# Two more pairs of down tiles as 2x2 block products in seven, on the first side of a fused attention and GLU block

## The chip, the cores and the metric

The kernel runs on one core of a Trainium2 chip. The metric is the device time of one execution in microseconds (us), as a median over several runs. One execution was also recorded by the hardware profiler; its rows give every instruction's start and duration. Engines are named as in the profile: PE multiplies matrices (PEld loads its stationary operand), DVE and POOL do elementwise work, ACT does elementwise work with a scale or function and most copies out of PSUM, SP issues DMA transfers. Each engine takes its instructions strictly in the order in which they were written.

## The reference

x is 2048 tokens of 512 numbers, all in float32. What is computed, with `ln` a layer norm without weights:

```python
sa, ca, ga, sb, cb, gb = (silu(c) @ w_mod) in six rows of 512
h = ln(x) * (1 + ca) + sa
x = x + ga * linear_attention(h, wqkv, wo)        # 32 heads of 16, phi(t) = elu(t) + 1 + 1e-6
h = ln(x) * (1 + cb) + sb
x = x + gb * (((h @ w_gate) * (h @ w_up)) @ w_down)   # 512 -> 1376 -> 512
```

## The kernel before

**Products in three passes.** The matrix products run on a shortened float32 type. So an operand X is split into a high part (ACT rounds it) and a low part (DVE or POOL subtracts the high part from X), and a product is three matmuls: high by high, high by low, low by high. Each split is thus one ACT instruction and one subtraction.

**Two sides.** The tokens are four chunks of 512 (j = 0 to 3 are four tiles of 128 tokens in a chunk). The GLU part works on two chunks at a time: the first side is chunks 0 and 1, the second side chunks 2 and 3. The hidden dimension of 1376 is cut into eleven f tiles (ten of 128, the last of 96). A **stage** here is one call of `block` (L1050 on), for one side and one f tile: the gate and up products of two chunks are seen as a 2x2 block product and done in seven products instead of eight (Winograd's form). The seven are called a11, s1, s2, a12, s3, a22, s4 in the code's order, each of 6 matmuls of 128x512 (L1057). They run in four PSUM banks a to d that all stages use in turn. On the way ACT copies b out of a, c out of b, then u2 (from b), g (from a) and u3 (from c); DVE adds c22 = d + u3 (L1113) before s4 may accumulate into d, and c12 = d + u2 (L1122) behind s4, then multiplies gate by up (L1083, twice). So the next stage's s1, which overwrites d, waits for L1122, and its a22, which accumulates into c, waits for the copy u3 (L1063).

The first side's stages 0 to 10 take the f tiles 2, 3, 4, 5, 6, 7, 8, 9, 0, 1, 10 in this order (`groups_of`, `order`). They begin at 206 us of the span; the second side follows at 373 us.

**The down product, two ways.** Where a group of f tiles is not *paired*, each h is split (L206, L207), and `down` (L1137) multiplies it for one or two f tiles at a time: 24 matmuls of 128x512 in each stage of the following group (L1146 to L1148), into four banks of the pool `ps_acc`, from which DVE adds into x (L1153, 128x512). Where two f tiles are *paired*, two chunks by two f tiles are again a 2x2 block product in seven (`Pair` from L1165, `pair_steps`). Its left operands are a11, a21 (first f tile), a12, a22 (second) and four sums s1 to s4 of them (L1182), split in L1168 and L1172; its right operands are the two rows of w_down and four sums of them, made on POOL (L1207) from rows that DVE has scaled by gb (L1280), and split in L1217 (ACT) and L1218 (DVE on the first side). A pair's seven steps are done for j = 0, 1 and again for j = 2, 3, 84 matmuls of 128x256 in all (L1226). A step b starts from a copy of step a's bank that ACT makes (`seed`, L1063 acc<-acc), and after most steps DVE adds a 128x256 result into x (L1253). Before the change, only tiles 0 and 1 are paired on the first side, and all full tiles on the second.

**Order.** There is no scheduler: every engine runs in the order of the code. `at` names points between the seven products of a stage ("s1" is behind s1, "pe" and "mid" lie around a22, "s4" is behind s4), and lists of jobs are run at each: the loading, summing and splitting of the next f tile's gate and up weights (`right_load`; `right_sums`, L1002 on POOL; `right_split`, L1013 and L1016 on ACT and L1020 on POOL), the down work, `trickle` (preparation of the second side's operands: sums L953 on DVE, splits L206 and L207), and the table `early`, which holds the end of the attention part: `y_a`/`y_b` (output projection of token tiles 12 to 15, L871 and L881), `turned` (L846, L850, L854) and the layer norm of chunks 2 and 3 (`ln2_x` L277, `ln2_turn` transposes L284 into a `ps_acc` bank, `ln2_f` L925 on ACT, which empties that bank).

`ps_acc` has four banks; `y_a`, `turned`, `ln2_turn`, `down` and the pair steps all take from it. A new use takes the bank that was given free the longest ago in the code's order, and waits for its last reader.

Of the kernel before, what the change touches and what calls it, by code (L numbers as in the profile page):

```python
# [22 lines left out]
def tile_adaln_block(  # L23
# [50 lines left out]
    def B(tag, shape=(P, D), dt=F32):  # L74

        return T(tiles, tag, shape, dt)

    def acc_bank():
        return T(ps_acc, "acc")
# [155 lines left out]
    def cut(pair, a, b):  # L235
        return pair[0][:, a:b], pair[1][:, a:b]
# [605 lines left out]
    def turn_a(i, of=bank):  # L842
        tps[i] = of()
        phi = phq.pop(i)
        for k in range(KD):
            nc.tensor.transpose(tps[i][:, k * P:(k + 1) * P], phi[:, k * P:(k + 1) * P], ident)  # L846

    def turn_h(i):
        pqs[i] = (B("xh", dt=F32R), B("xl", dt=F32R))
        nc.scalar.activation(pqs[i][0], tps[i], AF.Copy)  # L850

    def turn_l(i):
        h, l = pqs[i]
        nc.vector.tensor_tensor(l, tps.pop(i), f32(h), op=ALU.subtract)  # L854
# [8 lines left out]
    def y_a(i):  # L863
        pq = pqs.pop(i)
        fresh = i not in seeded
        if fresh:
            yps[i] = acc_bank()
        for k in range(KD):
            (ah, al), (bh, bl) = cut(pq, k * P, (k + 1) * P), wp[k]
            for n, (x, y) in enumerate(((ah, bh), (ah, bl), (al, bh))):  # L870
                nc.tensor.matmul(yps[i], x, y, start=fresh and k + n == 0,  # L871
                                 stop=k == KD - 1 and n == 2, skip_group_check=True)

    def y_b(i):
        ch, j = divmod(i, NJ)
        ps = yps.pop(i)
        if i in seeded:
            nc.scalar.activation(xts[ch][j], ps, AF.Copy)
            norm2[ch].stats(j, of=ps)
        else:  # L880
            nc.vector.tensor_tensor(xts[ch][j], xts[ch][j], ps, op=ALU.add)  # L881
            norm2[ch].stats(j)
# [36 lines left out]
    def ln2_turn(ch, *ks, of=bank):  # L919
        norm2[ch].transpose(*ks, of=of)  # L920

    def ln2_f(ch, *ks):
        for k in ks:
            f = B("f")
            nc.scalar.activation(f, norm2[ch].ps[k], AF.Identity, scale=cb[:, k:k + 1], bias=sb[:, k:k + 1])  # L925
            norm2[ch].ps[k] = None
            if ch < 2:
                plain[ch, k] = f
            else:
                nc.sync.dma_start(kept[ch, k], f)  # L930
# [457 lines left out]
    def turned(i):  # L1388
        turn_a(i, of=acc_bank)
        turn_h(i)  # L1390
        turn_l(i)

    def ln2_x(ch, *js):
        norm2[ch].xhat(*js)

    def ln2_r(ch, a=0, b=NJ):
        norm2[ch].rstd_of(a, b, True)

    def ln2_m(ch, a=0, b=NJ):
# [12 lines left out]
        (1, "pe"): [lambda: y_a(14), lambda: y_b(14)],  # L1412
        (1, "mid"): [lambda: ln2_turn(2, 0, 1, of=acc_bank)],
        (1, "s4"): [lambda: ln2_f(2, 0, 1)],
        (2, "s1"): [lambda: turned(15), lambda: ln2_turn(2, 2, 3, of=acc_bank)],
        (2, "s2"): [lambda: ln2_f(2, 2, 3)],
        (2, "pe"): [lambda: y_a(15), lambda: y_b(15), lambda: ln2_r(3)],
        (3, "s2"): [lambda: ln2_x(3, 0)],
        (3, "s3"): [lambda: ln2_x(3, 1)],
        (3, "mid"): [lambda: ln2_x(3, 2)],  # L1420
        (3, "s4"): [lambda: ln2_x(3, 3)],
        (4, "s1"): [lambda: ln2_turn(3, 0, 1, of=acc_bank)],
        (4, "s2"): [lambda: ln2_f(3, 0, 1)],
        (5, "s1"): [lambda: ln2_turn(3, 2, 3, of=acc_bank)],
        (5, "s2"): [lambda: ln2_f(3, 2, 3)],
    }
# [4 lines left out]
    groups = groups_of[1]  # L1431
    tail = groups[-1][-1]
    POINTS = ("s1", "s1", "a12", "a12", "pe", "pe", "s4")
    paired = {(0, g) for g in [4]} | {(1, g) for g in range(len(groups))}
    pair_of = {(s, f): (s, g) for s, g in paired for f in groups_of[s][g][:2]}
    same = {(1, 0): (0, 4)}
    points = POINTS
# [3 lines left out]
    for n, (s, g, f) in enumerate(order):  # L1441
        groups = groups_of[s]
# [72 lines left out]
        if was and was[:2] in paired and was[2] == groups_of[was[0]][was[1]][1]:  # L1515
            of, p = was[0], pairs[was[:2]]
# [87 lines left out]
```

## Time and profile before

| | |
|---|---|
| runs: median (lowest to highest) | 553.79 us (553.67 to 554.7) |
| span of the profiled execution, first to last instruction | 552.4 us |
| median of the runs less that span | 1.4 us |
| PE busy | 545.8 us, 99% |
| DVE, ACT, POOL busy | 432.2, 299.5, 176.8 us |
| stage 1 (second tile of the first group) | 221.5 to 235.1 us |
| stage 4 and stage 5 | 269.1 to 285.0, 285.0 to 300.8 us |
| stage 6 and stage 7 | 300.8 to 315.8, 315.8 to 330.8 us |
| stages 9 and 10 (end of the one pair before, and what follows it) | 345.7 to 373.1 us |

Times in the profile are microseconds from the first instruction. In a row of the timeline stand the start, the duration (of all instructions that it merges, with their count behind the x), engine, line, what is written and read, the size, and in brackets the idle time of the engine just before with what ended it. PE instructions overlap in the records (a 128x512 matmul lasts 390 ns, but the next starts after some 227 ns), so what a matmul costs is read from starts.

### The profile page before, as it was taken

The page shows a single profiled execution, that of the slowest core. Times are in us where ns is not written, and L with a number is a line of the kernel's source. Part 1 is how long each engine was busy: PE and PEld are TensorE (multiplying, and loading weights), DVE is VectorE, ACT ScalarE, POOL GpSimd, SP SyncE. Part 2 cuts the span into 40 slices and gives each one's busy share as a digit, 9 for nine tenths or more (in the row PEclk, how much of TensorE's full clock was granted, in tenths as well). Part 3 has the DMA queues.
Part 4 walks back from the last instruction along what each step waited for, and adds up shares of the span by engine and source line. Part 5 has one row for each costly group of instructions (what it writes and reads, how often), then busy time and mean ns, then how long its engine had stood idle before and what let it go on. Part 6 is the DMA issues. An engine that isn't in the chain of part 4 may idle for free. (4 is left out here: it accounts for less than half of the span.)

```text
span 552.4 us, 8146 instructions
## 1 busy us (share of the span) xinstructions
PE 545.8 (99%) x2775; PEld 460.1 (83%) x2775; DVE 432.2 (78%) x794; ACT 299.5 (54%) x535; POOL 176.8 (32%) x180
## 2 busy tenths in 40 slices
PE   8999999999999999999999999999999999999997
PEld 6888888888888888888888888878888888888886
DVE  6878779978998998865655767797577877879696
ACT  4876857456467876654545355463243534453540
POOL 2000000003527646353556644540002524242400
PEclk9999999999999999999999999999999999999999
DMA  8910224203230045195888634289786534342004
GB/s 256 373 57 1 76 77 152 77 0 77 78 115 2 0 154 189 39 316 180 285 286 274 222 123 163 87 312 391 231 259 218 173 131 138 129 146 86 1 0 153
DMA packets 58512, 83.24 MB, mean 151 GB/s; under 512 B 6564, under 2 KB 23720, under 8 KB 58472
## 3 DMA queue, kind: packets, MB, share of 16 engines
q1 hardware_dynamic: 56544, 81.16, 44.1%
q10 hardware_dynamic: 1928, 1.58, 0.9%
q8 instruction: 22, 0.36, 0.3%
q14 instruction: 18, 0.15, 0.1%
HBM read 53.02 MB, written 29.69 MB: 150 GB/s over the span
## 5 line engine op out<-in xcount | busy, mean ns | idle before, releaser
L1057 PE MATMUL bank<-h,w 128*128 128x512 f32 (+1 forms) x924 | 221.6, 391 | 0.2 <-POOL w L1020 0.2
L1057 PEld LDWEIGHTS bank<-h,w 128*128 128x128 f32 (+1 forms) x924 | 168.2, 186 | 36.2 <-POOL w L1020 0.6
L1063 ACT ACTIVATE bank<-bank 128x512 f32<-128x512 f32 (+2 forms) x46 | 26.2, 571 | 122.7 <-PE bank L1057 122.5
L1253 DVE TENSOR_TENSOR x<-acc,x 128x256 f32<-128x256 f32 x132 | 48.0, 414 | 13.7 <-PE acc L1226 13.1
L1226 PE MATMUL acc<-w,kh 128*128 128x256 f32 x308 | 57.1, 282 | 0.0
L1226 PEld LDWEIGHTS acc<-w,kh 128*128 128x128 f32 x308 | 50.6, 190 | 3.7
L1020 POOL TENSOR_TENSOR w<-raw,w 128x256 fp32r<-128x256 f32 (+3 forms) x22 | 24.7, 1121 | 73.7 <-ACT w L1013 64.1
L219 PE MATMUL bank<-w,h 128*128 128x512 f32 x112 | 44.1, 394 | 0.0
L221 PE MATMUL bank<-w,h 128*128 128x512 f32 x112 | 43.7, 390 | 0.0
L220 PE MATMUL bank<-w,h 128*128 128x512 f32 x112 | 43.6, 390 | 0.0
L1226 PE MATMUL acc<-w,kl 128*128 128x256 f32 x154 | 43.5, 283 | 0.0
L871 PE MATMUL acc<-w,xh 128*128 128x512 f32 x128 | 40.7, 399 | 0.0
L712 POOL TENSOR_TENSOR f<-h,zb 128x512 f32<-128x512 f32 x12 | 17.5, 1468 | 62.9 <-ACT zb L692 48.9
L262 POOL TENSOR_TENSOR rstd<-ve,half 128x4 f32<-128x4 f32 (+3 forms) x12 | 11.2, 935 | 81.4 <-DVE ve L259 68.0
L1083 DVE TENSOR_TENSOR phi<-bank,g 128x512 f32<-128x512 f32 (+1 forms) x22 | 15.1, 687 | 25.2 <-PE bank L1057 25.2
L1063 ACT ACTIVATE u<-bank 128x512 f32<-128x512 f32 (+1 forms) x44 | 26.1, 594 | 15.4 <-PE bank L1057 15.2
L1113 DVE TENSOR_TENSOR g<-bank,u 128x512 f32<-128x512 f32 (+1 forms) x22 | 15.2, 689 | 21.2 <-ACT u L1063 19.9
L1020 POOL TENSOR_TENSOR w<-t,w 128x512 fp32r<-128x512 f32 (+1 forms) x22 | 29.6, 1346 | 0.0
L1146 PE MATMUL acc<-w,kh 128*128 128x512 f32 (+1 forms) x76 | 29.6, 390 | 0.0
L1147 PE MATMUL acc<-w,kh 128*128 128x512 f32 (+1 forms) x76 | 29.6, 390 | 0.0
L1148 PE MATMUL acc<-w,kl 128*128 128x512 f32 (+1 forms) x76 | 29.6, 389 | 0.0
L277 ACT ACTIVATE n<-x,nmr,rstd 128x512 f32<-128x512 f32 x31 | 23.6, 808 | 10.9 <-DVE nmr L267 10.7
(204 smaller groups left out, 1187.0 us busy)
## 6 DMA issues: line engine op xcount, KB each, us to landing
right<-w SPq DMA_DIRECT2D x56, 256.0 KB, 3.7
w<-right SPq DMA_DIRECT2D x56, 256.0 KB, 4.3
x<-in_A_x_dram SPq DMA_DIRECT2D x22, 256.0 KB, 5.2
raw<-in_w_mod_dram SPq DMA_DIRECT2D x22, 256.0 KB, 3.7
raw<-in_B_w_down_dram SPq DMA_DIRECT2D x18, 256.0 KB, 3.0
side_s<-h SPq DMA_DIRECT2D x16, 256.0 KB, 2.6
h<-side_s SPq DMA_DIRECT2D x16, 256.0 KB, 5.3
raw<-in_A_wqkv_dram SPq DMA_DIRECT2D x12, 256.0 KB, 6.2
```

What stands on the lines that cost most here:

```text
L219: nc.tensor.matmul(ps, ah, bh, start=begin and i == 0, stop=False)
L220: nc.tensor.matmul(ps, ah, bl, start=False, stop=False)
L221: nc.tensor.matmul(ps, al, bh, start=False, stop=end and i == n - 1)
L871: nc.tensor.matmul(yps[i], x, y, start=fresh and k + n == 0, stop=k == KD - 1 and n == 2, skip_group_check=True)
L1020: sub = lambda out, x, y: (on or nc.gpsimd).tensor_tensor(out, x, f32(y), op=ALU.subtract)
L1057: mm = lambda x, y, **kw: nc.tensor.matmul(ps, x[:, k], y, skip_group_check=True, **kw)
L1063: nc.scalar.activation(out, x, AF.Copy)
L1146: nc.tensor.matmul(dn[j], hh[:n, a:b], dh[:n], start=i == 0, stop=False)
L1147: nc.tensor.matmul(dn[j], hh[:n, a:b], dl[:n], start=False, stop=False)
L1148: nc.tensor.matmul(dn[j], hl[:n, a:b], dh[:n], start=False, stop=i == n_of - 1)
L1226: mm = lambda x, y, **kw: nc.tensor.matmul(ps, x[:, a:b], y, skip_group_check=True, **kw)
L1253: nc.vector.tensor_tensor(xt[:, halves[at]], banks[b][m], xt[:, halves[at]], op=ALU.add)
```

## The change

The set `paired` gains the groups 0 and 2 of the first side, f tiles 2, 3 and 6, 7. Their down products go from `down` to `Pair`. In `early`, `y_a(15)` moves from "pe" of stage 2 to "s3", the two sets of transposes of chunk 2 behind it from "s1" to "s3" with their `ln2_f` from "s2" to "pe", and the first two transposes of chunk 3 in stage 4 from "s1" to "pe" with their `ln2_f` from "s2" to "mid".

```diff
-        (2, "s1"): [lambda: turned(15), lambda: ln2_turn(2, 2, 3, of=acc_bank)],
-        (2, "s2"): [lambda: ln2_f(2, 2, 3)],
-        (2, "pe"): [lambda: y_a(15), lambda: y_b(15), lambda: ln2_r(3)],
+        (2, "s1"): [lambda: turned(15)],
+        (2, "s3"): [lambda: y_a(15), lambda: ln2_turn(2, 2, 3, of=acc_bank)],
+        (2, "pe"): [lambda: y_b(15), lambda: ln2_r(3), lambda: ln2_f(2, 2, 3)],
...
-        (4, "s1"): [lambda: ln2_turn(3, 0, 1, of=acc_bank)],
-        (4, "s2"): [lambda: ln2_f(3, 0, 1)],
+        (4, "pe"): [lambda: ln2_turn(3, 0, 1, of=acc_bank)],
+        (4, "mid"): [lambda: ln2_f(3, 0, 1)],
...
-    paired = {(0, g) for g in [4]} | {(1, g) for g in range(len(groups))}
+    paired = {(0, g) for g in [0, 2, 4]} | {(1, g) for g in range(len(groups))}
```

Three places show how the order moves. The first is DVE in stage 1. Before, from the scaling of one w_down row (raw) to c22 (L1113):

```order
L1280 TENSOR_TENSOR raw_2393<-raw_2393,row_1417 128x512
L207 TENSOR_TENSOR kl_2579<-phi_2533,kh_2578 128x512
L207 TENSOR_TENSOR kl_2583<-phi_2536,kh_2582 128x512
L854 TENSOR_TENSOR xl_2592<-acc_2586,xh_2591 128x512
L207 TENSOR_TENSOR w_2605<-raw_2393,w_2604 128x512
L1113 TENSOR_TENSOR g_2628<-bank_2390,u_2626 128x512
L718 TENSOR_REDUCE den_2163<-f_2521 128x32
```

The same stretch of the changed kernel (s is the sum s3, kl a low part of a left operand, w a low part of w_down, t the sums that POOL makes):

```order
L1182 TENSOR_TENSOR s_2577<-phi_2536,phi_2533 128x512
L1172 TENSOR_TENSOR kl_2580<-phi_2536,kh_2579 128x512
L854 TENSOR_TENSOR xl_2589<-acc_2583,xh_2588 128x512
L1280 TENSOR_TENSOR raw_2511<-raw_2511,row_1417 128x512
L1280 TENSOR_TENSOR raw_2513<-raw_2513,row_1417 128x512
L1172 TENSOR_TENSOR kl_2612<-s_2577,kh_2611 128x512
L1218 TENSOR_TENSOR w_2626<-raw_2511,w_2625 128x512
L1218 TENSOR_TENSOR w_2630<-raw_2513,w_2629 128x512
L1113 TENSOR_TENSOR g_2641<-bank_2390,u_2639 128x512
L1218 TENSOR_TENSOR w_2644<-t_2596,w_2643 128x512
L1218 TENSOR_TENSOR w_2648<-t_2597,w_2647 128x512
L718 TENSOR_REDUCE den_2163<-f_2521 128x32
```

Four instructions (L1280, three of L207) have become nine, and two of them come behind POOL's sums t. The rest of the stage, from L718 to L1122, stands as before.

The second place is ACT in stage 4. Before, from the `ln2_f` of the transposes (f out of acc) on:

```order
L925 ACTIVATE f_3147<-acc_3126,col_1268,col_1324 128x512
L925 ACTIVATE f_3150<-acc_3131,col_1268,col_1324 128x512
L1063 ACTIVATE u_3159<-bank_2388 128x512
L1063 ACTIVATE g_3161<-bank_2387 128x512
L1063 ACTIVATE u_3169<-bank_2389 128x512
L206 ACTIVATE h_3173<-f_2922 128x512
L206 ACTIVATE h_3181<-f_2924 128x512
L1013 ACTIVATE w_3189<-raw_2823 128x256
L1016 ACTIVATE w_3191<-t_3080 128x512
L1016 ACTIVATE w_3193<-raw_2826 128x512
L1016 ACTIVATE w_3195<-t_3081 128x512
```

Now:

```order
L1063 ACTIVATE u_3235<-bank_2389 128x512
L206 ACTIVATE h_3239<-f_2950 128x512
L206 ACTIVATE h_3247<-f_2952 128x512
L1013 ACTIVATE w_3255<-raw_2858 128x256
L1016 ACTIVATE w_3257<-t_3126 128x512
L1016 ACTIVATE w_3259<-raw_2861 128x512
L1016 ACTIVATE w_3261<-t_3127 128x512
L925 ACTIVATE f_3324<-acc_3276,col_1268,col_1324 128x512
L925 ACTIVATE f_3327<-acc_3281,col_1268,col_1324 128x512
```

The two L925 now stand behind the splits that follow u3. On PE the transposes into acc_3276 and acc_3281 stand directly before `down` of the stage, whose third and fourth bank (acc_3300, acc_3301) are the two banks of these transposes.

The third place is DVE in stage 6, behind the four L1153. Before:

```order
L953 TENSOR_TENSOR s_3434<-f_2920,f_3331 128x512
L1280 TENSOR_TENSOR raw_3089<-raw_3089,row_1417 128x512
L207 TENSOR_TENSOR kl_3475<-phi_3423,kh_3474 128x512
L207 TENSOR_TENSOR kl_3479<-phi_3426,kh_3478 128x512
L207 TENSOR_TENSOR w_3490<-raw_3089,w_3489 128x512
L1113 TENSOR_TENSOR g_3511<-bank_2390,u_3509 128x512
L953 TENSOR_TENSOR s_3513<-s_3357,f_2918 128x512
L953 TENSOR_TENSOR s_3515<-s_3359,f_2920 128x512
L1083 TENSOR_TENSOR phi_3579<-bank_2389,g_3511 128x512
```

Now (the first two L1182 are the pair's sums s1 and s2, the third is s4):

```order
L953 TENSOR_TENSOR s_3541<-f_2948,f_3418 128x512
L1182 TENSOR_TENSOR s_3593<-phi_3337,phi_3530 128x512
L1182 TENSOR_TENSOR s_3598<-s_3593,phi_3340 128x512
L1172 TENSOR_TENSOR kl_3596<-s_3593,kh_3595 128x512
L1172 TENSOR_TENSOR kl_3601<-s_3598,kh_3600 128x512
L1172 TENSOR_TENSOR kl_3584<-phi_3533,kh_3583 128x512
L1113 TENSOR_TENSOR g_3625<-bank_2390,u_3623 128x512
L953 TENSOR_TENSOR s_3627<-s_3464,f_2946 128x512
L953 TENSOR_TENSOR s_3629<-s_3466,f_2948 128x512
L1182 TENSOR_TENSOR s_3652<-phi_3533,s_3598 128x512
L1253 TENSOR_TENSOR x_127<-acc_3666,x_127 128x256
L1253 TENSOR_TENSOR x_129<-acc_3666,x_129 128x256
```

The sums of the pair stand between the trickle's L953. On ACT the high parts of s1 and s2 stand ahead of the copies u2, g and u3, and the high part of s4 ahead of the seed copy.

## The prediction, made before the changed kernel was run

> **What bounds the kernel now.** I read the page first (busy shares, slices, idle columns), then the stages as windows, then the timelines of single engines around each place that the change touches.
>
> ```profile
> span 552.4 us, 8146 instructions
> PE 545.8 (99%) x2775; PEld 460.1 (83%) x2775; DVE 432.2 (78%) x794; ACT 299.5 (54%) x535; POOL 176.8 (32%) x180
> ...
> L1253 DVE TENSOR_TENSOR x<-acc,x 128x256 f32<-128x256 f32 x132 | 48.0, 414 | 13.7 <-PE acc L1226 13.1
> L1226 PE MATMUL acc<-w,kh 128*128 128x256 f32 x308 | 57.1, 282 | 0.0
> ```
>
> ```profile
> core 0: us, PE busy (x) PEld busy (x) DVE busy (x) ACT busy (x) POOL busy (x), PEclk, DMA share, GB/s
> 221.50:235.10 13.60, 13.60 (x67) 11.35 (x66) 11.50 (x18) 9.63 (x17) 5.05 (x5) 1.00 0.15 40
> 235.10:254.20 19.10, 19.10 (x92) 15.93 (x92) 9.59 (x17) 8.01 (x15) 12.14 (x14) 1.00 0.98 328
> 254.20:269.10 14.90, 14.90 (x67) 12.36 (x66) 8.87 (x14) 10.03 (x18) 5.15 (x5) 1.00 0.45 149
> ...
> 300.80:315.80 15.00, 15.00 (x67) 12.39 (x67) 11.75 (x17) 6.17 (x12) 8.82 (x9) 1.00 0.76 273
> ...
> 461.30:476.00 14.70, 14.70 (x87) 12.97 (x86) 14.25 (x26) 6.27 (x11) 5.08 (x6) 1.00 0.48 161
> ```
>
> PE sets the end: it is busy 99% of the span, and in every stage quoted its busy time is the stage's length. So the time falls by what PE is spared, and rises by every gap that another engine tears into it. DVE is the nearest rival: 11.5 of 13.6 us in stage 1, 11.75 of 15.0 in stage 6. A stage with a pair can carry 14.25 of 14.7 us of DVE work without a gap, as the last row (second side) shows, but only if the work comes early enough.
>
> The profiled execution spans 552.4 us, and the median of the runs is 553.8, so 1.4 us lie around the span. I add changes of the span to 553.8.
>
> **What PE is spared.** The prices of the two kinds of matmul, from the timeline: 24 of `down`, first and last and what follows, then 12 of a pair step with what precedes and follows.
>
> ```profile
> 246.01 0.39 PE L1146 MATMUL acc<-w,kh 128*128 128x512 f32 x1
> ...
> 251.23 0.39 PE L1148 MATMUL acc<-w,kl 128*128 128x512 f32 x1
> 251.45 0.84 PE L1057 MATMUL bank<-h,w 128*128 128x512 f32 x3
> ...
> 434.78 0.40 PE L1226 MATMUL acc<-w,kh 128*128 128x256 f32 x2
> ...
> 436.21 2.91 PE L1057 MATMUL bank<-h,w 128*128 128x512 f32 x12
> 438.96 0.40 PE L1226 MATMUL acc<-w,kh 128*128 128x256 f32 x2
> ```
>
> From start to start, 24 take 251.45 - 246.01 = 5.44 us, 0.227 each; 12 take 436.21 - 434.78 = 1.43 us, 0.119 each. A group of two tiles costs 48 x 0.227 = 10.9 us before and 84 x 0.119 = 10.0 us now: 0.85 saved, 1.7 for two groups. Twelve of L1057 behind a pair step take 2.75 us, 0.03 above 12 x 0.227; with eight such seams a group I take 0.4 off. **PE gains 1.3 us** (1.2 to 1.7).
>
> [...]
>
> **What is added.** A group's DVE work before is 2 scalings, 2 + 4 splits and 8 adds of 512; now 2 scalings, 4 + 6 splits, 4 sums and 24 adds of 256. ACT gets five instructions more per group, POOL four sums and a split. DMA transfers are the same in number; SP meets the two `kept` stores of stage 4 later, with weight stores behind them that nothing reads for stages. `y_a(15)` and the transposes move within stage 2, where DVE is idle half the time, and I cost that at nothing (9.59 of 19.1 us busy; cover gone, one L925, about 0.7). Stage 3 has room too, and I take it that stages 5 and 8 do. Three places do not.
>
> **A. Stage 1, and s1 of stage 2.**
>
> ```profile
> 225.26 1.29 DVE L207 TENSOR_TENSOR kl<-phi,kh 128x512 fp32r<-128x512 f32 x2
> 226.46 0.69 DVE L854 TENSOR_TENSOR xl<-acc,xh 128x512 fp32r<-128x512 f32 x1
> 227.44 0.69 DVE L207 TENSOR_TENSOR w<-raw,w 128x512 fp32r<-128x512 f32 x1 [0.29 <-ACT w L206]
> 229.70 0.69 DVE L1113 TENSOR_TENSOR g<-bank,u 128x512 f32<-128x512 f32 x1 [1.57 <-ACT u L1063]
> ...
> 231.01 1.07 DVE L735 TENSOR_TENSOR den<-den,den 128x32 f32<-128x32 f32 x1
> ...
> 235.34 0.69 DVE L1122 TENSOR_TENSOR g<-bank,u 128x512 f32<-128x512 f32 x1
> ...
> 233.68 4.35 PE L1057 MATMUL bank<-h,w 128*128 128x512 f32 x18
> 237.87 0.60 PE L846 MATMUL acc<-ident,h 128*128 128x128 f32 x4
> ...
> 352.48 1.28 DVE L1280 TENSOR_TENSOR raw<-raw,row 128x512 f32<-128x512 f32 x2
> ...
> 358.24 1.51 DVE L1218 TENSOR_TENSOR w<-t,w 128x512 fp32r<-128x512 f32 x2 [2.07 <-ACT w L1217]
> ```
>
> The 18 matmuls are s4 of stage 1, a11 and s1 of stage 2; s1 starts 6 x 0.227 before 237.87, at 236.51. It overwrites d, which L1122 frees at 236.03: a reserve of 0.48 us. DVE gets nine instructions for four ahead of L1122. Back to back one takes 0.60 (two from 225.26 to 226.46), so 3.0 us more. Idle are 0.29 + 1.57 = 1.86 us. Were all of it filled, s1 would wait 3.0 - 1.86 - 0.48 = 0.7; were none, 2.5. What decides is that the last two splits wait for POOL's sums and ACT's copies of them. The pair in stage 9 has the same queue, and there, 5.8 us behind the scalings, DVE still stood idle 2.07 us for t. In stage 1 the scalings can't start before about 226.5, so t is ready late in the 231s. I take 2.0. POOL's work shifts by 2 to 3 us, so it may meet more of DVE's: L735, a 32-column add, took 1.07 us beside POOL. Another 0.6 at the upper end: **0.7 to 3.1, taken 2.0.** Behind L1122 stand the products of the stage and `turned(15)`; y_a(15) needs these 8 us later, so nothing more is late.
>
> **B. Stage 4: banks 3 and 4 of `down`.**
>
> ```profile
> 277.60 0.62 ACT L1063 ACTIVATE u<-bank 128x512 f32<-128x512 f32 x1
> 278.07 1.18 ACT L206 ACTIVATE h<-f 128x512 fp32r<-128x512 f32 x2
> 279.11 0.45 ACT L1013 ACTIVATE w<-raw 128x256 fp32r<-128x256 f32 x1
> ...
> 279.94 0.66 ACT L1016 ACTIVATE w<-raw 128x512 fp32r<-128x512 f32 x1
> 280.46 0.66 ACT L1016 ACTIVATE w<-t 128x512 fp32r<-128x512 f32 x1
> ...
> 275.32 1.44 ACT L925 ACTIVATE f<-acc,col,col 128x512 f32<-128x512 f32 x2
> ```
>
> From the start of u3 to the end of the last split are 281.12 - 277.60 = 3.5 us; the first L925 (half of 1.44) then ends 4.2 us behind u3's start. u3 can start 0.2 us after PE has issued s3. PE goes on with eight transposes (0.8) and 12 matmuls (2.7), and needs the bank at 3.5 us: a gap of 4.4 - 3.5 = 0.9. Where ACT's splits run at 0.52 from start to start (279.94 to 280.46) with less in their way, 0.4. **0.4 to 1.0, taken 0.8.**
>
> **C. Stages 6 and 7.** Here the trickle's L953 stand between the pair's sums. For the sums I use stage 10, which follows the only pair of this side.
>
> ```profile
> 304.86 1.28 DVE L953 TENSOR_TENSOR s<-f,f 128x512 f32<-128x512 f32 x2
> ...
> 309.51 2.73 DVE L953 TENSOR_TENSOR s<-s,f 128x512 f32<-128x512 f32 x2
> ...
> 307.64 0.39 PE L1146 MATMUL acc<-w,kh 128*128 128x512 f32 x1
> ...
> 365.26 1.34 DVE L1182 TENSOR_TENSOR s<-phi,phi 128x512 f32<-128x512 f32 x1
> 366.64 0.69 DVE L1182 TENSOR_TENSOR s<-s,phi 128x512 f32<-128x512 f32 x1
> ...
> 370.09 0.68 DVE L1182 TENSOR_TENSOR s<-phi,s 128x512 f32<-128x512 f32 x1
> ...
> 368.86 0.59 ACT L1063 ACTIVATE u<-bank 96x512 f32<-96x512 f32 x1
> ...
> 371.34 0.58 ACT L1063 ACTIVATE acc<-acc 128x512 f32<-128x512 f32 x1
> ```
>
> First, u3. Nothing changes on DVE up to the L953 that end at 306.14. Two sums at 0.60 end at 307.3. In stage 10 u3 ends 369.45 - 367.33 = 2.1 us behind the second sum, since ACT makes two high parts, u2 and g before it: 309.45 here. PE has s3 out at 307.64 (there `down` starts now) and two pair steps, 1.44, so it wants a22 at 309.1: it waits 0.4, or 1.9 with sums 1.38 apart as in stage 10.
>
> Second, the seed. L1113 follows u3 and ends its turn at 310.1; then come the two L953, 2.73 us in this very place beside POOL's splits (1.2 if free), then the sum s4, whose end is at 313.4 (312.0). In stage 10 the seed copy ends 371.92 - 370.77 = 1.15 us behind that sum: 314.6 (313.1). PE, having started a22 at 309.5, is through s4 at 312.2 and waits for the seed 2.4 us (0.9).
>
> Third, bank b. Before step s3 of the pair may write into it, DVE must have added step s2 to x, and seven instructions of 0.60 and four adds of some 0.34 stand between the sum s4 and that: 5.7 us. PE needs 0.72 + 1.36 + 1.36 + 0.72 = 4.2 us from the seed: 0.3 more, up to 1.0.
>
> Together 0.4 + 2.1 + 0.3, a little under the measured 2.73 in the second: **1.6 to 5, taken 2.8.**
>
> **The sum.** -1.3 + 2.0 + 0.8 + 2.8 = +4.3 us: 553.8 + 4.3 = **558.1 us**. All low ends: -1.7 + 0.7 + 0.4 + 1.6 = +1.0, 554.8. All high ends: -1.2 + 3.1 + 1.0 + 5.0 = +7.9, 561.7.
>
> **Rivals.** (1) *DVE and ACT keep up, and only PE's saving is left:* 553.8 - 1.3 = 552.5. For it: second-side stages bear 14.25 us of DVE work without a gap, and a gap in stage 2 gives all engines time. Against it: those stages have no L953, no attention work, and POOL's sums there come with time to spare. It decides if L1122 of stage 1 ends within 0.48 us of its old place and the seed of stage 6 is there before s4 is through. Chance 0.11. (2) *Only one of the three gaps opens, at its low end,* say the seed's 0.9 with B's 0.4: -1.3 + 1.3, no change: 553.8. [...] Against it: 2.73 for two L953 is measured, not supposed. Chance 0.08. (3) *DVE becomes the bound from stage 5 on:* the scalings and four splits there also push the L953 behind stage 5's end, s1 of stage 6 waits about 1, and C goes to 5: 558.1 + 1.0 + 2.2 = 561.3 or above. For it: L953 in stage 5 come last on DVE. Against it: they waited for a DMA there, so nine instructions for four find cover. Chance 0.12. (4) *The gaps appear but a later wait on the first side is shortened by as much:* before, PE waits nowhere in stages 3 to 9, so there is nothing to give back; within the forecast.
>
> **How the numbers follow.** Forecast 0.69, rivals 0.11, 0.08, 0.12. 0.2%, or 1.1 us, is about what a measurement of this kernel can tell from no change: faster is below 552.7, slower above 554.9. Rival 1 gives most of faster: 0.11. Same: rival 2 and the forecast's lower tip, 0.09. Slower: 0.80. The likeliest case's own range is 554.8 to 561.7. The range reaches down to 554.0, into rival 2, and up to 561.5: below it lie 0.15, above it 0.05.
>
> **What would show it.** In the changed profile: 84 x 2 more of L1226 and 96 fewer of L1146 to L1148; stages 3 and 7 at 14.6 us but for gaps (right step for PE). A: PE idle before s1 of stage 2, ended by DVE L1122. B: PE idle inside `down` of stage 4, ended by ACT L925. C: idle before a22 of stage 6 (ACT u3), before step s2 (ACT seed L1063), before step s3 in stage 7 (DVE L1253). If PE shows no gap of 0.5 us between 235 and 335 us, the forecast is wrong and rival 1 is right. If there are gaps elsewhere, above all before s1 of stage 6, rival 3.

## The result, and the profile after

The changed kernel takes **575.97 us** (median of 4 runs, 574.11 to 576.89) against 553.95 us for the kernel before beside it (4 runs, 553.67 to 554.7): a ratio of **1.039, 95% interval 1.0368 to 1.0412**. It is slower, as forecast, but by 22 us and not by 4.3; the range ended at 561.5. The profiled execution spans 573.6 us, 21.2 more than before. From its page:

```profile
span 573.6 us, 8370 instructions
PE 553.2 (96%) x2847; PEld 465.6 (81%) x2847; DVE 463.5 (81%) x842; ACT 308.0 (54%) x549; POOL 191.6 (33%) x190
...
PEclk9999999999999999899999889999999999999999
...
L1226 PE MATMUL acc<-w,kh 128*128 128x256 f32 x420 | 79.1, 285 | 8.9 <-DVE x L1253 6.3
...
L1253 DVE TENSOR_TENSOR x<-acc,x 128x256 f32<-128x256 f32 x180 | 65.4, 414 | 15.6 <-PE acc L1226 14.9
```

Before, PE had one gap of 0.2 us (stage 10) in the first side's stages and none else; now L1226 alone shows 8.9 us of idle time. A second thing is new: three slices with an 8 in the row of the granted clock. PE's busy time *rose* by 7.4 us although its work fell. The view of PE's waits over the first side, 205 to 396 us of the changed kernel, lists who ended them (total, times, longest, in us):

```profile
PE acc L1226 <- DVE x L1253: 6.3, 4, 2.9
PE bank L1057 <- DVE g L1122: 3.9, 3, 2.8
PE acc L1226 <- ACT acc L1063: 2.2, 2, 1.6
PE bank L1057 <- ACT u L1063: 0.8, 1, 0.8
PE acc L1146 <- ACT f L925: 0.6, 1, 0.6
PE acc L1226 <- ACT kh L1168: 0.4, 1, 0.4
PE acc L1226 <- DVE kl L1172: 0.2, 1, 0.2
```

That is 14.4 us of idle PE. Since the records overlap, a gap costs about 0.17 us more than the idle time that they show: measured from start to start, the 13 gaps cost 16.7 us. The stages 2, 3, 4, 6, 7 and 8 of the changed kernel as windows (columns as in the prediction: length, busy time of PE, PEld, DVE, ACT, POOL, clock, DMA):

```profile
235.00:255.40 20.40, 17.62 (x85) 14.47 (x84) 16.42 (x26) 10.09 (x19) 15.21 (x16) 0.92 0.64 215
255.40:271.80 16.40, 15.20 (x87) 12.92 (x87) 11.51 (x22) 9.99 (x19) 5.83 (x6) 1.00 0.59 212
271.80:293.20 21.40, 19.68 (x100) 15.94 (x99) 12.00 (x21) 9.25 (x17) 13.17 (x14) 1.00 0.68 225
...
309.10:327.40 18.30, 14.59 (x62) 11.19 (x61) 17.34 (x23) 8.03 (x15) 12.30 (x12) 0.91 0.48 164
327.40:346.30 18.90, 16.63 (x86) 14.01 (x85) 13.63 (x25) 7.83 (x15) 6.75 (x7) 0.91 0.38 143
346.30:367.60 21.30, 18.42 (x93) 15.29 (x92) 13.04 (x22) 9.35 (x18) 12.42 (x12) 1.00 0.47 156
```

In every one PE's busy time is now below the stage's length, by 1.2 to 3.7 us. Stages 5, 9 and 10 and the whole second side have no gap. In stage 6 DVE is busy for 17.34 of 18.30 us. And in stages 2, 6 and 7 the mean clock is 0.91 to 0.92. Four short windows of the same execution tell more:

```profile
239.20:242.60 3.40, 3.35 (x10) 2.69 (x11) 1.55 (x2) 1.15 (x2) 2.24 (x3) 0.50 1.06 406
...
321.10:324.50 3.40, 3.40 (x9) 2.64 (x8) 3.40 (x3) 1.02 (x2) 3.40 (x3) 0.50 0.00 0
334.80:338.20 3.40, 3.40 (x10) 2.65 (x8) 1.64 (x4) 1.60 (x3) 0.00 (x0) 0.51 0.00 0
353.10:356.50 3.40, 3.40 (x18) 2.96 (x19) 2.40 (x6) 1.08 (x3) 0.00 (x0) 1.00 0.00 0
```

Three times PE runs at half clock for 3.4 us, a 128x512 matmul every 0.427 us and not every 0.227 (starts at 239.81 and 240.24), some 5.1 us lost in all, half of 3 x 3.4. The sum: 16.7 of gaps, 5.1 of half clock, about 1.2 for the matmul behind each gap (0.1 us longer than others: two of L1226 take 0.50 us at 353.03, and 0.40 within a step), less the 1.3 spared, is 21.7, against 21.2 measured.

### The profile page after: what moved, and what is told of

Read it like the earlier page. It is cut to its first block, busy times and chain, and to the rows that moved or that the text cites. A ratio compares the mean times of both kernels' runs of the same rounds, so it can differ in the third digit from the quotient of the medians.

```text
span 573.6 us, 8370 instructions
## 1 busy us (share of the span) xinstructions
PE 553.2 (96%) x2847; PEld 465.6 (81%) x2847; DVE 463.5 (81%) x842; ACT 308.0 (54%) x549; POOL 191.6 (33%) x190
## 4 chain that ended last, share of the span: by engine, by line
PE 79%; issue 6%; DVE 6%; POOL 4%; ACT 3%; DMA 1%; POOLq 0%; ACTq 0%; DVEq 0%
PE bank L1057 28%; PE acc L1226 11%; PE acc L871 6%; PE bank L219 5%; PE bank L221 5%; PE bank L220 5%; POOL w L1020 3%; PE acc L372 3%; PE acc L374 3%; PE acc L373 3%; PE bank L284 2%; PE acc L459 2%; PE acc L1146 1%; PE acc L1147 1%; PE acc L1148 1%
## 5 line engine op out<-in xcount | busy, mean ns | idle before, releaser
L1057 PE MATMUL bank<-h,w 128*128 128x512 f32 (+1 forms) x924 | 229.1, 398 | 4.8 <-DVE g L1122 3.9
L1057 PEld LDWEIGHTS bank<-h,w 128*128 128x128 f32 (+1 forms) x924 | 170.1, 189 | 42.1 <-issue 4.2
L1226 PE MATMUL acc<-w,kh 128*128 128x256 f32 x420 | 79.1, 285 | 8.9 <-DVE x L1253 6.3
L1226 PEld LDWEIGHTS acc<-w,kh 128*128 128x128 f32 x420 | 68.6, 190 | 16.0 <-DVE x L1253 7.2
L1253 DVE TENSOR_TENSOR x<-acc,x 128x256 f32<-128x256 f32 x180 | 65.4, 414 | 15.6 <-PE acc L1226 14.9
L1226 PE MATMUL acc<-w,kl 128*128 128x256 f32 x210 | 59.5, 283 | 0.2 <-DVE kl L1172 0.2
L1020 POOL TENSOR_TENSOR w<-raw,w 128x256 fp32r<-128x256 f32 (+3 forms) x22 | 25.9, 1176 | 61.9 <-ACT w L1013 59.8
L1226 PEld LDWEIGHTS acc<-w,kl 128*128 128x128 f32 x210 | 40.0, 190 | 0.4 <-DVE kl L1172 0.4
L1168 ACT ACTIVATE kh<-s 128x512 fp32r<-128x512 f32 x32 | 19.9, 629 | 22.6 <-DVE s L1182 22.3
L1020 POOL TENSOR_TENSOR w<-t,w 128x512 fp32r<-128x512 f32 (+1 forms) x22 | 31.8, 1443 | 0.0
L1172 POOL TENSOR_TENSOR kl<-phi,kh 128x512 fp32r<-128x512 f32 x8 | 12.4, 1551 | 51.0 <-ACT kh L1168 47.4
L1113 DVE TENSOR_TENSOR g<-bank,u 128x512 f32<-128x512 f32 (+1 forms) x22 | 15.1, 687 | 16.2 <-ACT u L1063 16.2
```

Source lines behind the costliest of these rows:

```text
L1020: sub = lambda out, x, y: (on or nc.gpsimd).tensor_tensor(out, x, f32(y), op=ALU.subtract)
L1057: mm = lambda x, y, **kw: nc.tensor.matmul(ps, x[:, k], y, skip_group_check=True, **kw)
L1168: nc.scalar.activation(self.h[n][0], self.f[n], AF.Copy)
L1226: mm = lambda x, y, **kw: nc.tensor.matmul(ps, x[:, a:b], y, skip_group_check=True, **kw)
L1253: nc.vector.tensor_tensor(xt[:, halves[at]], banks[b][m], xt[:, halves[at]], op=ALU.add)
```

## The experiments

Each run gives a median beside runs of the kernel before on the same chip; spans are those of the profiled execution. Two readings ran through them. **T:** each gap is its own queue with its own remedy. **D:** DVE as a whole has no time left, and what it needs includes its waiting for POOL (**P** where this part alone is meant).

### Groups alone, and the order alone

In the table of pairs, the first keeps only tiles 2 and 3, the second only 6 and 7, the third neither (so that only the changed order stands):

```
-    paired = {(0, g) for g in [0, 2, 4]} | ...
+    paired = {(0, g) for g in [0, 4]} | ...      # group0
+    paired = {(0, g) for g in [2, 4]} | ...      # group2
+    paired = {(0, g) for g in [4]} | ...         # order_only
```

> Only tiles 2, 3 are paired in addition (group 0); tiles 6, 7 stay with down; the moved order stays. Theory (each gap of the changed kernel belongs to the DVE or ACT queue of the stages behind one pair): the gaps of stages 2 to 4 stay (2.9 before s1 of stage 2 with 1.9 of half clock behind it, four of about 0.75 in stages 3 and 4, 0.8 in down of stage 4), those of stages 6 to 8 vanish; less 0.65 spared: about 8 us above the kernel before, 562. Rival (one common cause, such as the moved order or too few buffers for everything together): the gaps of stages 2 to 4 shrink by more than half, or gaps stay in stages 6 to 8.

> Only tiles 6, 7 are paired in addition (group 2); tiles 2, 3 stay with down; the moved order stays. Theory: no gap before s1 of stage 2, 0.8 in down of stage 4, and the gaps of stages 6, 7 and 8 as in the changed kernel (0.8, 1.9, 1.8, 2.4, 3.0 and 3.4 of half clock): about 14 us above the kernel before, 568. Rival: stages 6 to 8 were late because DVE had been late since stage 2; then they lose less than half of this, and the run is below 561.

> The moved order of y_a(15) and of the two sets of transposes alone; paired as in the kernel before. Theory: one gap of 0.8 inside down of stage 4, which waits for ACT L925: 554.8. Rival (the order is the main loss): 558 or above. Rival (ACT is earlier with fewer splits): no gap, 553.9.

Measured: 562.86 us (ratio 1.0156, 1.0136 to 1.0176; span +8.6), 570.19 us (1.0288, 1.0245 to 1.0331; span +14.1) and 555.25 us (1.0024, 1.0014 to 1.0034; span +0.9). In the spans, 8.6 + 14.1 - 0.9 = 21.8, against 21.2 for both: within the scatter the groups do their damage independently (the two runs of group 2 lie 3.9 us apart, 568.24 and 572.15, and the profile is of the first). With group 0 alone, the gaps of stages 2 to 4 are as in the changed kernel, down to the 0.8 us inside `down`; with group 2 alone, those of stages 6 to 8. The order alone opens only that one gap, 0.79 us at 279.5 us of its span, ended by ACT's L925.

### Idle PE filled with matmuls that nobody reads

```
+    def fill(n):
+        ps, x = acc_bank(), side["a11"][0][0]
+        for _ in range(n):
+            nc.tensor.matmul(ps, x[:, :P], x, start=True, stop=True)
+    early[(2, "a11")] = [lambda: fill(12)]
```

> The changed kernel with 12 more matmuls of 128x512, whose product nobody reads, between a11 and s1 of stage 2, where PE stands idle for 2.8 us; they take 12 x 0.227 = 2.7. If the half clock behind this gap comes from the idle time, s1 and the matmuls behind it run at 0.227 again and 1.9 us are won: 574. Rival (the clock falls for another reason, or the fill delays s1): 576 or above.

Measured: 577.99 us (1.0429, 1.0408 to 1.045). That execution had lost some 4 us before stage 0 began, in a part that the edit does not touch; from the start of stage 0 it needs 366.3 us, against 367.7. The half clock in stage 2 was gone (s1 takes 1.46 us, not 2.70), though s1 still came behind L1122. So this slow stretch came with PE's idleness and not with the wait. By its median this run falls on the rival's side; by its trace stages 2 and 3 took 1.7 us less, as the first reading had it, and stage 8 1.7 us more. In stage 6 the half clock was gone too, but the wait for the seed copy grew from 1.8 to 3.4 us, and the stage took 18.1 instead of 18.3: **a PE that came earlier only waited longer where DVE set the pace.**

### One queue relieved at a time

The splits of group 0's right operands (L1217 and L1218; the expectation names other lines) one stage later, the trickle's work of stages 5 and 6 in stages 7 to 9 (its loads, not shown in the cut, at the end of stage 6), and both. `later` names the group 0 of the first side:

```
-  for x, ms in ((...) if s else ((("a12", (0, 1)), ("s3", (2, 3))))):
+  for x, ms in ((...) if s else () if (s, g) in later else ((("a12", (0, 1)), ("s3", (2, 3))))):
+  if was[:2] in later:                          # split_later, both_later: one stage on
+      at["s2"].append(lambda p=p: p.weight_splits(0, 2, on=nc.vector))
+      at["s3"].append(lambda p=p: p.weight_splits(1, 3, on=nc.vector))
...
-  at["s3"].append(lambda: some(2)); at["s4"].append(lambda: some(2 if n > 4 else 0))
+  TRICKLE = {3: (("s3", 2),), 4: (("s3", 2),), 7: (("mid", 2), ("s3", 2), ("s4", 2)),
+             8: (("mid", 2), ("s3", 4), ("s4", 2)), 9: (("a12", 4),)}     # trickle_later, both_later
```

> Edit: the four splits of the first pair's right operands (ScalarE line 1013 and VectorE line 1020), made in stage 1 so far, are made in stage 2: two behind s2, two behind s3; nothing else. Theory T (each gap has its own cause in the queue of VectorE or ScalarE at that place, and the half clock comes behind a gap that is long enough): the gap of 2.9 us before s1 of stage 2 goes, and with it the half clock behind it (1.9 us); all the gaps of stages 3, 4 and 6 to 8 stay within 0.5 us: about 571 us (570 to 572.5). Rival R1 (the first pair's extra work on VectorE as a whole is too much, wherever it stands): the gap moves, s3 or the pair's products of stages 2 and 3 wait as long: 574 to 577 us.

> Edit: the second side's left operands (sums and splits, lines 953 and 207) that were made in stages 5 and 6, two behind s3 and two behind s4 of each, are made in stages 7, 8 and 9, and their loads are issued at the end of stage 6; as many instructions in all. Theory T: the gaps of stage 6 (0.8 before s1, 0.9 inside step d, 1.0 before a22, 1.8 before step s2, 1.7 half clock) and of stage 7 (2.4, and 1.6 half clock) mostly go; stage 8's gap of 3.0 stays unless it was handed on from stage 6: some 10 to 13 us less, 563 to 567 us. Rival R1 (the pair's extra work is too much for VectorE in any order): the waits turn up in stages 8 and 9 and the first stages of the second side: 572 us or more.

> Edit: the two edits before this one together. Theory T: the savings add, 4.8 + 10 to 13: 558 to 562 us, the gaps of stages 3 and 4 (0.76 twice, 0.67, 0.76, 0.78) stay. Rival R1: 570 us or more.

Measured: 577.02 us (1.0414, 1.0393 to 1.0435), 575.62 us (1.0389, 1.0368 to 1.0409) and 575.94 us (1.0394, 1.0373 to 1.0415). Not one is clearly faster than the changed kernel, and where T had said 563 to 567 and 558 to 562 us for the last two: **T fell.** (With the splits moved to these places the kernel no longer computes the whole result: part of the output is off, for a reason that was not settled. It still runs the changed kernel's matmuls and splits.) What became of the gap that split_later removed is seen in DVE's timeline of stage 2:

```profile
246.46 0.69 DVE L1113 TENSOR_TENSOR g<-bank,u 128x512 f32<-128x512 f32 x1 [0.17 <-ACT u L1063]
248.84 1.71 DVE L1218 TENSOR_TENSOR w<-raw,w 128x512 fp32r<-128x512 f32 x1 [1.69 <-ACT w L1217]
250.47 1.75 DVE L1218 TENSOR_TENSOR w<-t,w 128x512 fp32r<-128x512 f32 x1
252.14 0.68 DVE L881 TENSOR_TENSOR x<-x,acc 128x512 f32<-128x512 f32 x1
```

DVE waits 1.69 us for ACT's high part, which stands behind the splits of the next right tile there, then needs 1.7 us for each subtraction, and only then adds the y product to x, for whose bank a pair step waits: 5.8 us of idle PE, where 2.8 had been before s1. In trickle_later stages 6 and 7 together took 28.2 us and not 37.2, but stages 8, 9 and 10 took 55.6 and not 48.1. Its PE waits:

```profile
PE bank L1057 <- DVE g L1122: 8.0, 4, 3.9
PE acc L1226 <- DVE x L1253: 3.4, 4, 1.5
PE bank L1057 <- DVE g L1113: 1.4, 1, 1.4
```

The longest, 3.9, is the one before s1 of stage 2, which this edit does not touch and which was 2.8. DVE's timeline shows the same instructions in both, with one pair of them longer; the row below is trickle_later's:

```profile
232.44 2.96 DVE L1218 TENSOR_TENSOR w<-t,w 128x512 fp32r<-128x512 f32 x2
```

In the changed kernel that row is 1.81 us (below). **The same two instructions took 1.1 us more, in a stretch where DVE's work and POOL's stand side by side.**

### Stage 4's copy ahead of the splits

```
-        (4, "pe"): [lambda: ln2_turn(3, 0, 1, of=acc_bank)],
-        (4, "mid"): [lambda: ln2_f(3, 0, 1)],
+        (4, "s3"): [lambda: ln2_turn(3, 0, 1, of=acc_bank), lambda: ln2_f(3, 0, 1)],
```

> Edit: the kernel with the changed order alone (tiles 2, 3, 6, 7 as single tiles), with stage 4's two transposes and their copies by ScalarE (line 925) moved from before a22 and behind it to the front of the work behind s3. Theory T: the 0.78 inside the down products of stage 4, the one gap that the order alone opened, is ScalarE's copy behind the splits of the next right tile (L1013); it goes, and the time is that of the kernel before within 0.1%, 553.6 to 554.3 us, where the order alone gave 555.25. Rival R2 (the 0.8 is the bank itself: three banks of acc in turn cannot take transposes and two jobs of down in one stage wherever they stand): 555.0 to 555.6 us.

Measured: 554.72 us (1.0022, 1.0005 to 1.0038; 10 runs, 553.98 to 558.49), span 552.8 us. The gap is gone from the trace and the span is within 0.4 us of the kernel before; the runs scatter too widely to tell the median from either expectation.

### Work left out of DVE, of POOL, of both

```
+  if on is None: nc.gpsimd.tensor_tensor(l, ...)   # no_wlow: the first side's pairs read h for l
+  else: l = h
...
+  l = h                                            # no_rlow: Right.lows reads h for l from stage 1 on
```

> Leaves out the low parts of the first side's pairs' right operands (VectorE, line 1218: four instructions each in stages 1, 5 and 9); TensorE reads the high part in their place, so it has the same matmuls, and ScalarE the same copies. Theory D (VectorE's queue is what every gap hangs on, since one pair puts about 4.2 us of splits into stages 1 and 5, in front of what the next stage waits for): the wait before s1 of stage 2 and its half clock go (4.8 us), the wait before s1 of stage 6 (0.8) goes, and of the later waits of stages 6 to 8, which were found behind instructions that VectorE started late, the greater part goes too: 556 to 563 us. Theory T (each gap has its own place): only the first two go, 569 to 571 us. Rival R3 (ScalarE's queue is the one that is late): 574 us or more.

> Leaves out GpSimd's subtractions for the low parts of the single right tiles from stage 1 on (line 1020, three of 128x512 per stage); TensorE reads the high part in their place: the same matmuls, the same VectorE and ScalarE instructions, and 3.8 to 5.2 us less of GpSimd per stage. Theory P (VectorE's instructions with both operands in SBUF wait for a GpSimd instruction under way, 0.68 becomes 1.1 to 1.8): VectorE's four splits of stage 1 take 0.68 each in place of 1.06 on average, line 747 1.2 or less, so that the wait before s1 of stage 2 falls from 2.8 to about 0.6 with no half clock behind it; with the same in stages 5 to 8 a sum of 562 to 568 us. Rival R4 (the contention is a side show, VectorE's own work is what is too long): the durations fall, but the time stays at 573 us or more.

> Leaves out both sorts of low parts: VectorE's for the first-side pairs' right operands (line 1218) and GpSimd's for the single right tiles (line 1020) from stage 1 on; TensorE reads the high parts in their place, with the same matmuls. Theory D+P (the loss is VectorE's time: its own added work, and what it waits for GpSimd): the wait of 3.0 before s1 of stage 2 and the half clock behind it, which leaving out line 1020 alone did not touch, go as they went without line 1218; ScalarE's late copies stay in stages 3, 4 and 6 (0.76, 0.78, about 0.5 and 1.7): 554.5 to 557 us. Rival T (the two act on the same waits): 560 us, no better than without line 1020 alone.

> The kernel before with the low parts of line 1020 left out in the same way (TensorE reads the high parts): a control. Theory D+P: before, VectorE's waits for GpSimd were all under the cover of TensorE, which never stopped, so that nothing is won: 553.3 to 554.3 us. If it is 551 us or less, leaving out line 1020 saves something by itself, and the 14 us that it saved in the changed kernel are not all contention.

Measured: without DVE's splits 569.55 us (1.0272, 1.0242 to 1.0302), without POOL's subtractions **561.25 us** (1.0122, 1.0093 to 1.0152), without both **557.95 us** (1.0067, 1.0044 to 1.009), and the control 554.15 us (1.0004, 0.9985 to 1.0023). (These kernels have 3 or 6 lines more from the edit on: L1256 and L1229 in no_rlow are L1253 and L1226.) Without POOL's low parts, PE waits for:

```profile
PE bank L1060 <- DVE g L1125: 3.0, 1, 3.0
PE acc L1229 <- ACT acc L1066: 2.2, 2, 1.6
PE acc L1229 <- DVE x L1256: 0.9, 1, 0.9
PE acc L1149 <- ACT f L925: 0.6, 1, 0.6
PE bank L1060 <- ACT u L1066: 0.4, 1, 0.4
```

and without both:

```profile
PE acc L1232 <- ACT acc L1066: 1.6, 2, 1.0
PE acc L1232 <- DVE x L1259: 1.4, 2, 0.7
PE acc L1149 <- ACT f L925: 0.6, 1, 0.6
PE bank L1060 <- ACT u L1066: 0.5, 1, 0.5
```

Leaving 27 instructions out of POOL, an engine that is busy a third of the time, takes 14.7 us off the changed kernel and nothing off the kernel before. The wait for DVE's adds falls from 6.3 to 0.9, the gaps from 16.7 to 8.3 us, and no half clock is left, which is 5.1 us of the 14.7. The same 842 DVE instructions are busy for 451.5 us and not 463.5; in the kernel before the same edit takes only 4.7 us off DVE's 432.2. P's figure for stage 1 was a miss: the wait before s1 of stage 2 stayed at 3.0. The six L1218 that read POOL's sums took 962 ns on average and not 859; the likely reason, not shown by itself, is that POOL, with less to do, went on to its next sums beside them. Leaving out DVE's splits takes the waits for L1122, that one among them, and its 569.55 us lie in T's range and not in D's: DVE's own added splits are the smaller part. In no_both the two savings add for the most part, 18.0 us together against 6.4 + 14.7 = 21.1. no_both came out 0.9 us above its expectation: two waits for DVE's adds stayed at 0.7 us each.

### POOL's and DVE's work exchanged

```
-  p.weight_splits(*ms, on=None if s else nc.vector)
+  p.weight_splits(*ms, on=None if s or p is not pairs.get((0, 4)) else nc.vector)   # pool_splits
...
+  at["a11"].insert(0, lambda p=p: p.weight_splits(0, 2))                            # pool_later: one stage on,
+  at["s1"].insert(0, lambda p=p: p.weight_splits(1, 3))                             # on POOL
...
-  at["s3"].append(lambda n=n: right_split(n + 1))
+  at["s3"].append(lambda n=n: right_split(n + 1, nc.vector if 5 <= n <= 7 else None))  # dve_rlow
```

> Edit: the low parts of the right operands of the two new pairs (line 1218's subtractions of stages 1 and 5) are made by GpSimd and not by VectorE, in the same places of the program; nothing is left out. Theory D: the waits before s1 of stages 2 and 6 go, but GpSimd has 5.1 us more in stages 1 and 5, ahead of the low parts of the next right tile (line 1020), for which a11 of stages 2 and 6 would then wait some 1 to 3 us: 564 to 572 us. [...]

> Edit: the splits of the right operands of the two new pairs are moved out of stages 1 and 5 to the front of stages 2 and 6 (two behind a11, two behind s1), and their subtractions from VectorE to GpSimd, which is idle from 2 us after stage 2's start for about 5 us; nothing is left out. Theory D: the waits before s1 of stages 2 and 6 go, and VectorE's work of stages 2 and 6 to 8 starts earlier, the late copies of ScalarE in stage 6 stay: 558 to 566 us. Theory T: 568 to 571 us. Rival R1 (the work turns up as a wait elsewhere, as it did when the first pair's splits went behind s2 and s3): 574 us or more.

> The changed kernel with line 1020's subtractions of stages 5 to 7 (four in each) made by VectorE and not by GpSimd; nothing is left out. Theory P (a GpSimd subtraction of 128x512 beside a busy VectorE costs VectorE about 1.05 us, more than the 0.68 it would need for that work itself): VectorE's queue gains (1.05 - 0.68) times 9 and loses 0.68 times 9 where there was no collision, so a small gain or none in stage 6, 570 to 576 us. Theory D alone (VectorE's own work is the bound, the contention is nothing): 9 times 0.68 and 3 times 0.41 more, 7.4 us: 580 to 584 us.

Measured: DVE's eight splits given to POOL in place 575.36 us (1.0377, 1.0347 to 1.0407), one stage later 574.78 us (1.0366, 1.0336 to 1.0396): no gain, although DVE has eight instructions fewer, and not where D had put them (564 to 572 and 558 to 566); the second lies where R1 had it, at 574 or more. In pool_splits PE waits 1.9 us for POOL's L1020 in stage 2, and 5.5 us for seed copies. Twelve subtractions given from POOL *to* DVE, in the stages where DVE is fullest: **573.5 us** (1.0349, 1.0319 to 1.0379), no slower, where by its expectation DVE's own work alone would have made it 580 or more. DVE's groups by line in stages 5 to 7, first of the changed kernel, then of dve_rlow (count, busy us, mean ns):

```profile
L953 DVE TENSOR_TENSOR s<-f,f 128x512 f32<-128x512 f32 x4 | 5.6, 1427 | 0.0
...
L953 DVE TENSOR_TENSOR s<-s,f 128x512 f32<-128x512 f32 x2 | 2.7, 1396 | 0.0
```

```profile
L1020 DVE TENSOR_TENSOR w<-t,w 128x512 fp32r<-128x512 f32 x6 | 4.1, 682 | 0.0
L953 DVE TENSOR_TENSOR s<-f,f 128x512 f32<-128x512 f32 x4 | 3.6, 950 | 0.0
...
L953 DVE TENSOR_TENSOR s<-s,f 128x512 f32<-128x512 f32 x2 | 1.3, 682 | 0.0
```

What DVE takes over costs it 682 ns apiece, and the sums around it fall from 1427 and 1396 ns to 950 and 682. This run also had 3.9 us before s1 of stage 2 instead of 2.8; stages 3 to 10 take 136.0 us here and 139.0 in the changed kernel. Those 3.0 us are not less waiting: the gaps of stages 3 to 10 add up to 14.2 us here and 13.7 there, and what is gone are the two stretches of half clock in stages 6 and 7, some 3.4 us. So the exchange is about even: by these rows, what DVE takes over costs it roughly what it had lost beside POOL.

No version beats the kernel before. The most that the pairs can bring is PE's 1.3 us (2 by the sums below), and even with 39 instructions left out, 5.1 us of gaps remain.

## Why the prediction was wrong

**The cause.** The sign was right and the size was not: DVE's work was costed mostly at the durations that it has when POOL is out of its way, and packed closer it meets POOL more often. The gaps priced in A, B and C were 5.6 us; measured are 16.7: A 2.9, B 0.8, C 6.1, the wait before s1 of stage 6 0.8, and 6.0 in stages 3, 4 and 8, where nothing was priced. Half clock (5.1) and the slower matmul behind each gap (1.2) come on top. Here are DVE in stage 6 and POOL in the same microseconds, in the changed kernel's timelines:

```profile
320.90 2.72 DVE L953 TENSOR_TENSOR s<-s,f 128x512 f32<-128x512 f32 x2
323.54 1.76 DVE L1182 TENSOR_TENSOR s<-phi,s 128x512 f32<-128x512 f32 x1
325.23 0.74 DVE L1253 TENSOR_TENSOR x<-acc,x 128x256 f32<-128x256 f32 x2
...
328.45 2.37 DVE L953 TENSOR_TENSOR s<-f,s 128x512 f32<-128x512 f32 x2
330.74 1.21 DVE L1280 TENSOR_TENSOR raw<-raw,row 128x512 f32<-128x512 f32 x1
```

```profile
235.15 1.29 POOL L1020 TENSOR_TENSOR w<-raw,w 128x512 fp32r<-128x512 f32 x1
...
321.35 1.72 POOL L1020 TENSOR_TENSOR w<-t,w 128x512 fp32r<-128x512 f32 x1
323.03 1.73 POOL L1020 TENSOR_TENSOR w<-raw,w 128x512 fp32r<-128x512 f32 x1
```

The pair's sum L1182 takes 1.76 us beside POOL subtractions of 128x512; another L1182 of the same size, with no POOL instruction near it, takes 0.69. Beside POOL's 128x256 sums (L1002) the scaling L1280 takes 1.21 and not 0.68. POOL's own instruction takes 1.73 in place of 1.29 (the first row, from stage 2). The adds L1253, which read one operand from PSUM, keep their 0.41 in every stage. So on this side DVE's work on two SBUF operands took longer beside POOL's, and a stage with POOL busy for 12 to 15 us had less room for DVE than its idle share told. The runs without POOL's low parts bear it out: the same DVE instructions, busy 12.0 us less. The 14.7 us of time are not contention alone: besides the half clock, waits for the end of POOL's subtractions go with them (stages 4 and 8, below).

By the prediction's steps:

- **PE's saving: right in the counts.** 84 x 2 more of L1226 and 96 fewer in `down`. No run shows the saving by itself. The sums of gaps and half clock overshoot the spans of the changed kernel, no_rlow and no_both by 0.5 to 0.8 us, so PE may have been spared as much as 2 us, not 1.3.
- **A, taken 2.0, bounds 0.7 to 3.1: 2.9, ended by L1122 as said.** Of the 1.86 us of idle DVE, 1.1 stayed idle (0.39 and 0.73), and the four splits lost time to POOL (L747 took its 1.33 before, too):

```profile
229.44 2.25 DVE L1218 TENSOR_TENSOR w<-raw,w 128x512 fp32r<-128x512 f32 x2 [0.73 <-ACT w L1217]
...
232.22 1.81 DVE L1218 TENSOR_TENSOR w<-t,w 128x512 fp32r<-128x512 f32 x2
...
235.66 1.33 DVE L747 SCALAR_TENSOR_TENSOR h<-h,den 128x512 f32<-128x512 f32 x1
...
238.45 0.66 DVE L1122 TENSOR_TENSOR g<-bank,u 128x512 f32<-128x512 f32 x1
```

  The four splits take 2.25 and 1.81 us, where two took 1.28 in stage 9 of the kernel before (L1218): 1.5 us more. The contention's 0.6 stood only in the upper bound. The wait fell inside the bounds here, but in two other runs of the same code it was 3.9: the bound was too narrow.
- **B, taken 0.8: 0.78,** inside `down` of stage 4, ended by ACT's L925. The order alone has it, order_early takes it away: shown.
- **C, taken 2.8, bounds 1.6 to 5: 6.1, the mechanism right, the size not.** u3 before a22 1.0 (0.4 taken) and 0.9 more inside step d, which was not priced; the seed 1.8 (2.1 taken); bank b in stage 7, taken 0.3 and at most 1.0, **2.4**. The seven instructions and four adds up to that point, priced at 5.7 us (7 x 0.60 and 4 x 0.34 are 5.6), took 7.9 (325.30 to 333.21): three ran at 1.2 beside POOL, and DVE stood idle 0.5 us for a POOL instruction's end.
- **Rival 3 (0.12) was the nearer one.** The 0.8 us before s1 of stage 6 is there, and DVE is the bound, 17.34 of 18.30 us in stage 6. Even it ended at "561.3 or above", as it kept the prices.
- **The failed step: "Stage 3 has room too, and I take it that stages 5 and 8 do".** The pairs' steps run on into stages 3, 4 and 8, and PE waits there as well: in stage 3 0.76 us for bank b and 0.76 for the seed, in stage 4 0.67 before s1 and 0.76 for bank b, in stage 8 3.0 for bank b. Idle DVE time is no cover for work that a step waits for in a fixed order. Nor is all of this delay DVE's own work. Three rows of the changed kernel:

```profile
272.51 0.69 DVE L1083 TENSOR_TENSOR phi<-bank,g 128x512 f32<-128x512 f32 x1 [2.46 <-POOL w L1020]
...
347.04 0.69 DVE L1122 TENSOR_TENSOR g<-bank,u 128x512 f32<-128x512 f32 x1 [1.80 <-DMA side_s<-h]
...
348.38 1.15 ACT L206 ACTIVATE h<-s 128x512 fp32r<-128x512 f32 x2 [2.93 <-POOL w L1020]
```

  None of the three reads what the instruction named behind the arrow made. All SBUF buffers of this kernel are taken in turn (`T` at L70), so the likely reason, not shown by itself, is that each is to write into a buffer that the other still reads. The first row holds up L1122 and with it s1 of stage 4: in no_rlow neither this wait nor stage 4's gaps of 0.67 and 0.76 are there. The other two come before stage 8's gap: DVE stands 1.80 us until a store of the trickle to DRAM is done, and its next splits (L207) need ACT's high part, for which ACT stands 2.93 us until POOL's L1020 ends. How the 3.0 us divide is open. With group 2 alone and in fill the store's wait is gone, ACT's is 3.37, and the gap is 3.4; in dve_rlow both long waits are gone and the gap is 2.6; in no_rlow they are gone too, with POOL's subtractions, and it is 1.0.
- **Never priced: the half clock**, 5.1 us, and the matmuls behind the gaps, 1.2.

Two things stay open: how the 14.7 us of no_rlow divide between POOL's contention and waits for POOL's end, and how far ACT's late copies (in no_both 0.6 and 1.0 us of idle PE for the two seeds, 0.6 for L925) are ACT's own queue. They stay when DVE's and POOL's low parts are left out, but only L925 was tried by itself.

## What to carry to other kernels

A busy share of 78% on the second engine isn't room: count what of its work takes longer beside another engine (here, what reads two operands from SBUF: 1.76 us beside POOL's subtractions, 0.69 without), take the durations of rows in which both are busy, and look whether the work is due in a fixed order. When moving a piece of work only moves the gap, look at the sum of the work, and an experiment that leaves work out finds it sooner than one that shifts it. And the price of the gaps on TensorE was here the gaps, 16.7 us, and what the clock did behind them, 5.1 us.

## What the runs showed of the hardware that was not expected

**Half clock behind some gaps and not behind others.** In the changed kernel it begins at 239.2, 321.1 and 334.8 us and lasts 3.4 us each time. It follows 2.8 us of idle PE before s1 of stage 2, before 321.1 only 1.4 us in three pieces (0.35, 0.23, 0.84), and before 334.8 one gap of 2.3. But 2.9 us in stage 8 left the clock at 1.00 (the last of the four windows above), and so did 3.0 us in no_rlow. So the length of a gap does not decide. Nor does the idle time within the last 3.4 us: 317.7 to 321.1 held 1.4 us of it and half clock followed, but 324.5 to 327.9 and 348.4 to 351.8 held 1.65 and 1.66, and none followed (1.00 from 327.9 to 331.3 and from 351.8 to 355.2). What decides isn't settled.

**Two prices for one program.** With instructions unchanged in stages 1 and 2, the wait before s1 of stage 2 was 2.8 or 3.9 us. POOL's first L1020 took 1.29 us beside DVE's last two splits in the changed kernel (these took 1.81), and 0.74 in trickle_later (these took 2.96); that it hangs on which engine's instruction goes first is the likely reason, not shown by itself. Differences of a microsecond between kernels with such a place say little.
